# A fused attention and FFT-convolution kernel whose written-out order is searched anew, with two table evacuations ordered and unit columns set early

## The chip, the cores and the metric

The kernel runs on one core of a Trainium2 chip. The metric is the device time of one execution in microseconds. Engines go by the profile's names: PE multiplies matrices (PEld loads its weights), DVE, ACT and POOL are the vector, scalar and general engines, SP only issues transfers. Most executions of one kernel agree within 0.3%, and the comparisons made here tell 2% from no change.

## The reference

Two stages. The first is attention with 8 global keys and a causal window of 96 keys, for 4 batches of 8 heads, 768 positions and 64 columns a head. The second takes the joined heads as 768 x 512 rows, projects them to three parts, convolves the middle part along the positions (a Fourier transform of 768 points, a product with the transform of a filter, the inverse), multiplies it by the two other parts and projects once more.

```python
scores = scale * np.matmul(q, k.transpose(0, 1, 3, 2))
scores = np.where(keep, scores + bias, -1e9)          # bias: -slope of the head * distance
a = softmax(scores)
x = np.matmul(a, v)                                   # heads joined: 4 x 768 x 512
x1, x2, x3 = np.split(x @ w_proj, 3, axis=-1)
x2_conv = irfft(rfft(x2, axis=1) * rfft(filter, axis=0), n=768, axis=1)
out = (x1 * x2_conv * x3) @ w_out
```

## The kernel before

`graph` builds a list of 1,025 operations with what each reads and writes; `ORDER` is a text that says, in one sequence for all engines, which operation comes next, on which engine (P, A, V, G, S for PE, ACT, DVE, POOL, SP) and in which of the eight PSUM banks its result lies. "231A" is operation 231 on ACT; "226P2" is operation 226 on PE in bank 2; "i20b1" is 20 dummy matmuls (512 columns each) into bank 1, which only occupy PE. Each engine runs its own operations strictly in that order. A text that is once written is not changed at run time: where something is late, everything behind it on that engine is late.

The order was found off line by a search with the costs in the list (`act`, `dve`, `pe` and single figures in microseconds). These costs steer nothing when the kernel runs. The dependencies in the list (`r` and `w` are names of what is read and written) restrict the search; the waits in the program come from the recording layer, which compares the memory that operations touch.

Stages, by batch b of four. `attention(b)`: PE turns q and k around (`turned`; for b = 0 q is turned in f32 straight from the loaded rows, `turned32`, L628), ACT or DVE move the results to QT and KT, PE makes scores of two heads at a time into two banks (`scores`, L672 and L681), ACT takes the exponential (L695), DVE multiplies by a mask for b > 0 (L712); for b = 0 PE adds the distances first, from the small tables near and slope (L672). PE multiplies by v (`values`, L730 and L735; v carries one column of ones behind its 64, so the sum of the weights falls out), DVE divides (rc L759, xn L754), PE turns the result (L775), ACT or DVE move it to xT. `gate` projects x1 and x3 from xT (L844). `butterfly` adds and subtracts thirds of xT on DVE. `conv(b)`: `conv` projects (L911), `spectra` transforms (L615) and multiplies by h1 and h2, the inverse (L936, L939) gives eo, DVE joins the parts, gates them, and PE makes the output (L963), which SP stores. Batch b + 1's attention is interwoven with batch b's convolution.

Things made once. `tables` makes angles on PE and sines on ACT (`fwd`). `inverse_tables` turns these with PE into one bank and evacuates it in six parts, i = 0 to 5: three into `inv`, whose columns interleave (i = 0 takes the even blocks, i = 1 and 2 the odd ones), one into the first half of `inr`, and two into the second half of `inr`, i = 4 for rows 0 to 63 and i = 5 for rows 64 to 127, with opposite signs. `spectrum` makes h1 and h2 from the filter: DVE sums thirds of the loaded filter (pp, L557 and on) and PE transforms. `distances` and `masks` make near, slope and the masks from tables of POOL (iota, select) and from its identity matrix.

Loads. SP loads q of batch 0 (six loads, 256 KB each in f32, into the output buffers ot) and the first v rows. POOL issues every other load, 81 in all: k and v of every batch in seven pieces each, q of batches 1 to 3 in six, the weights w and wo and the filter. `load_v` sets the column of ones (and 31 columns behind it) of the v buffer once for each of the two buffers; `load_first` does it for the first one.

In the order before, operation 231 (i = 4) is ACT's and 232 (i = 5) is DVE's:

```
178P1 179V 200V 207V 201V 208V 209V 233V 203V 234V 144P4 226P2 228A 227A 232V 235V 145P5 147A 231A 146A 148V
```

Of the kernel before, what the change touches and what calls it, by code (L numbers as in the profile page):

```python
# [39 lines left out]
0V 30V 7V 47S 48S 14S 16S 57S 15S 49S 17G 18G 21G 22V 27V 28V 5G 6A 46A 31A 32A 25A 40A 34A 44A 33A 60G 23G  # L40
70V 71A 77A 72A 43A 37A 41A 38A 35A 76A 39A 73A 9V 54G 53G 59G 66G 55G 58G 20G 257G 56G 19G i20b1 108P0 109V
i1b2 85P1 86V 8V 10V 24V 258G 63G 64G 62G 3G 61G i2b3 79P2 80V 26V 11V 83P3 84A 45A 42A 110P4 111V 29V 88P5
89V 260S 259G 256G 65G 67G 69G 255G 273G 268G 267G 154P0 160P2 161V 87V 13V i1b6 81P1 82A 36A 78A 112P4 113V
155V 114P2 115V 50V 270G 269G 68G 263G 276G 158P3 159V 12V 90P67 91A 92P45 93A 118P01 119A 116P67 117A 156P2
157V 52V 51V 261S 274G 271G 120P45 121A 96P23 97A 122P01 94P67 95A 123A 358P4 359V 4V 487G 266G 275G i1b5
124P23 125V 126V 162P45 163A 166P67 167A 103P01 104V 105V 129P23 130V 131V 219P4 220A 127P5 128A 74A 98P67 99V
100V 221V 262V 222V 264S 265S 164P01 165A 168P23 169A 214P5 215A 75A 132P6 101P7 102V 1V 133V 216V 170P01 171V
172V 106P4 107A 223A 360P7 175P23 176V 217V 218A 2A 177V 134P4 136V 173P6 174V 139P0 141V 149P5 151A 361A
178P1 179V 200V 207V 201V 208V 209V 233V 203V 234V 144P4 226P2 228A 227A 232V 235V 145P5 147A 231A 146A 148V
225V 210V 202V 211V 204V 135P6 137A 138V 212V 205V 140P7 191P3 193A 356P5 357A 229A 486G 508G 272G 488G 490S  # L50
185P6 150P4 152A 230A 196P3 198A 368P01 369A 362P45 190P2 192A 142A 363A 180P3 182V 236V 430P0 431A 384P1 385V
206V 213V 143V 153V 194V 237V 386P7 387A 499G 502G 498G 496G 485G 495G 489G 181P2 365P45 366A 186P3 188A 187A
183A 285P0 286V 238V 388P45 389A 224A 390V 239V 364V 367V 298P1 294P3 295A 299A 283P0 284A 371P67 372A 373V
391P45 392A 394P23 395A 296P1 297V 393V 281P0 434P6 435A 505G 497G 309P7 310A 282A 432P4 433V 491S 503G 277G
278G 279G 504G 195P1 197A 374P23 375V 370V 376V 189V 184V 244P5 245A 397P67 398A 242P0 243A 240P1 241V 399V
307P4 308A 287P5 288A 377P2 378A 379P67 380V 381V 246P3 247A 400P01 401V 396V 402V 289P4 290A 248P67 249A 250V
251V 252P23 254A 253A 302P5 303A 405P01 406V 291V 407V 442P67 443A 436P23 437A 300P4 301V 584P5 585A 403P6
404V 614P7 382P0 383V 444V 311V 292V 408P1 409A 445P23 446A 615A 447V 293V 588P6 716G 713G 492G 493S 718S 727G
717G 507G 720G 439P45 440A 586P0 587V 312V 438V 304V 441V 305V 411P1 416P2 418A 413A 612P3 420P7 422A 613A
589A 421P4 662P2 663A 423A 415P5 417A 453P01 454V 455V 410P3 412A 448P67 449V 450V 729G 714G 734G 501G 733G  # L60
724G 715G 726G 500G 280G 723G 725G 660P2 719S 494S 722S 721S 732G 506G 321P4 322A 661A 456P5 457V 658P3 659V
306V 199V 730G 735G 731G 736G 728G 599P01 600A 590P67 591A 451P4 452V 317P5 318V 479V 478V 419V 480V 424V 481V
426P3 425P2 427A 428A 319P4 320A 327P5 328A 625P01 626A 325P2 326A 468P3 323P4 324A 315P5 316A 459P6 461A
313P7 314V 482V 429V 483V 329V 330V 484V 331V 627V 332V 601V 333V 619P01 513P4 514A 620A 474P5 476A 470A 526P2
527A 593P67 596P01 597A 594A 598V 334V 336V 592V 337V 595V 509P4 524P5 525A 522P3 523A 464P2 466A 616P01
622P67 623A 617A 473P3 475V 511P2 512A 812P5 813A 510A 469P6 471A 842P7 843A 607P01 608V 414V 609V 624V 621V
335V 618V 458P5 350P4 351A 814P2 815A 460A 535P3 602P67 603V 604V 477V 472V 528P0 529A 536A 353P4 354A 347P5
537P2 538A 348A 349S 633P01 634V 635V 462V 530P3 531A 816P4 817A 605P2 628P67 629V 539V 532V 606V 533V 630V
610P3 611A 463P5 465A 673P01 674A 338P4 339A 344P5 345V 540V 667P23 668A 664P01 665A 631P4 632V 669V 467V 666V
534V 675V 341P6 342V 343S 352S 355S 346S 340S 636P7 637A 517P5 518A 670P23 671A 672V 818P01 819A 515P4 516A  # L70
653P7 888P5 889A 655A 676P23 677V 520V 678V 519V 820V 521V 890P0 886P1 638P6 640A 643P4 555P7 556A 887A 645A
840P5 841V 644P6 646A 679P7 680A 891A 681P23 682V 683V 647V 648P1 650A 541P6 542A 649P7 651A 553P2 554V 684P6
685V 707V 706V 824P45 825A 827P01 828A 545P7 543P3 544A 691P6 693V 546V 709V 708V 639P2 641A 642V 710V 829V
652V 711V 847P45 892P01 893A 848A 894V 702P3 704A 551P2 549P6 550A 552A 697P7 821P01 822A 823V 898P45 741P3
742A 699A 692P2 547P6 548A 899A 557V 558V 712V 826V 849V 559V 737P0 738A 686P3 688A 895P67 853P45 854A 694A
654P1 656A 754P0 755A 896A 830P45 831V 560V 832V 561V 562V 564V 563V 657V 752P3 753A 750P2 751A 844P01 901P67
902A 845A 850P45 851A 739P3 696P2 687P6 689A 833P7 834A 835P01 836V 565V 837V 846V 852V 855V 900V 765P4 766A
756P5 757A 740A 569P6 570A 701P7 703A 758P0 763P1 764A 759A 698A 856P45 857V 858A 743P3 744V 897V 903V 695V
575P6 861P01 862V 863V 745P7 746A 576A 577S 904P23 905V 906V 767V 838P4 839A 572P5 859P7 860A 909P01 910V 760V
761V 748V 768V 762V 690V 747V 864P4 865A 911A 578P6 907P7 882P4 872P2 874A 573A 574S 566P3 912P0 913V 908V  # L80
749V 934V 935V 936V 937V 938V 939V 700V 940V 581P2 582A 771P5 772A 884A 881P1 783P2 773P7 774A 784A 777P0
769P5 775P4 776A 778A 770A 781P7 867P2 779P4 780A 579A 958P0 959A 782A 785V 786V 705V 787V 788V 789V 790V 791V
792V 929P5 941P4 942A 869A 943P0 944A 567A 568S 571S 580S 583S 956P6 967P2 968A 957A 954P0 955A 871P3 945P4
946A 883A 885V 793V 877P2 879A 962P0 963A 960P4 947P1 948A 961A 964V 965V 794P2 876P0 969P1 970A 971V 966V
972V 866P7 949P4 950A 873A 878A 868A 951V 952V 953V 870V 875V 880V 930P1 932A 931A 933V 800P6 801A 924P3 979P0
975P7 976A 980A 988P1 989A 795A 796S 803P4 977P5 978V 973P0 974A 981V 982V 983V 992P1 993A 990P2 991A 986P6
987A 804A 994V 984V 995V 985V 996V 805S 797P0 798A 999V 997V 1000V 998V 1001V 1002V 799S 802S 919P2 809P1 810A
921A 926A 811S 806P5 807A 1014V 808S 915P0 920P4 922A 917A 923V 914P2 916A 918V 1012V 925P3 927A 928V 1013V
1015V 1006P1 1007A 1008S 1003P2 1004A 1005S 1009P3 1010A 1011S 1022P0 1023A 1024S 1016P1 1017A 1018S 1019P2
1020A 1021S  # L90
"""


class Bank:


    def __init__(self):
# [1128 lines left out]
```

## Time and profile before

| | |
|---|---|
| median of 3 runs (lowest, highest) | 180.44 us (179.66, 183.96) |
| the profiled execution, its own time | 182.07 us |
| its span, first to last instruction | 180.3 us |
| mean granted PE clock | 0.986 |
| busy: PE, DVE, ACT, POOL | 168.0, 158.1, 153.7, 76.0 us |
| instructions | 4465 |
| POOL's transfer queue: packets, share of 16 DMA engines' span | 80912, 92.5% |

The profile is of one execution. Busy is the time in which an engine has an instruction in it; instructions of one engine may overlap by some hundredths, and PE's ends are modelled, so the distance from start to start of PE instructions says more than their durations. A row of the timeline has start, duration, engine, line, operation, what is written and read, and in brackets how long the engine stood idle and what ended that. The waits have total, times and longest. A line can be that of a helper: L307 and L311 are all of `copy` and `times` on ACT and DVE, so the names of the tiles tell operations apart.

### The profile page before, as it was taken

To read this page: it belongs to the slowest core of one execution; us is meant where nothing else is said; L and a number is where in the kernel's file an instruction comes from. 1 tells how busy PE (TensorE), PEld (TensorE's weight loads), DVE (VectorE), ACT (ScalarE), POOL (GpSimd) and SP (SyncE) were. 2 spreads that over 40 slices of the span, in tenths; PEclk is the share of its full clock that TensorE was granted. 3 is DMA by queue.
4 is the path that set the end of the run, shared out by engine and by line. 5 is a ranking of instruction groups with operands and counts; after the bars stand their busy time and mean duration, and the time that the engine had idled before them with its cause. 6 is when DMAs were issued, how large, how long until landed. Compare 5 with 4: busy or idle time off the path is not lost.

```text
span 180.3 us, 4465 instructions
## 1 busy us (share of the span) xinstructions
PE 168.0 (93%) x1725; PEld 105.8 (59%) x1725; DVE 158.1 (88%) x352; ACT 153.7 (85%) x298; POOL 76.0 (42%) x97
## 2 busy tenths in 40 slices
PE   7957997959999999999999999999999999999990
PEld 2545786634645576874476567665557674566540
DVE  2899889995698999999999999898999999999930
ACT  2697997938899999997999898899998888789761
POOL 7999998297895809899940000000000000000000
PEclk9999999996999999999999999999999999999998
DMA  6999999999999989999999106000001010501744
GB/s 122 208 177 164 161 165 204 175 178 157 161 138 109 133 54 66 138 142 143 164 151 71 58 26 268 4 0 0 4 0 63 20 39 25 210 4 58 291 184 167
DMA packets 91133, 20.74 MB, mean 115 GB/s; under 512 B 83864, under 2 KB 88040, under 8 KB 91112
## 3 DMA queue, kind: packets, MB, share of 16 engines
q0 software_dynamic: 80912, 12.14, 92.5%
q1 hardware_dynamic: 10200, 8.31, 14.6%
q8 instruction: 13, 0.21, 0.5%
q14 instruction: 8, 0.07, 0.1%
HBM read 25.84 MB, written 6.29 MB: 178 GB/s over the span
## 4 chain that ended last, share of the span: by engine, by line
PE 76%; DVE 15%; ACT 3%; issue 3%; POOL 2%; POOLq 0%; ACTq 0%; DVEq 0%
PE bank L844 21%; PE bank L911 12%; PE bank L963 12%; PE bank L681 6%; PE bank L936 5%; PE bank L641 5%; PE bank L615 4%; PE bank L775 3%; PE bank L730 3%; PE bank L735 3%; PE bank L672 2%; DVE xn L754 2%; DVE pp L557 1%; PE bank L939 1%; DVE eo L307 1%
## 5 line engine op out<-in xcount | busy, mean ns | idle before, releaser
L844 PE MATMUL bank<-xT,w 128*128 128x384 f16 x256 | 50.6, 332 | 2.5 <-ACT g L854 2.5
L695 ACT ACTIVATE E<-bank 128x864 f16<-128x864 f32 x48 | 41.1, 910 | 2.1 <-PE bank L681 2.0
L844 PEld LDWEIGHTS <-w 128*128 128x128 f16 x256 | 23.7, 99 | 18.5 <-issue 4.5
L323 POOL DMA_DIRECT2D kn<-in_k_dram x28 | 25.7, 920 | 9.4 <-PE bank L641 6.1
L323 POOL DMA_DIRECT2D vn<-in_v_dram x28 | 25.9, 927 | 4.9 <-DMA g<-in_moe_filter_fft_dram 3.0
L963 PE MATMUL bank<-wo,y 128*128 128x512 f16 x96 | 23.3, 379 | 0.0
L712 DVE TENSOR_TENSOR E<-E,mask 128x864 f16<-128x864 f16 x36 | 20.9, 597 | 0.0
L754 DVE TENSOR_TENSOR xn<-bank,rc 128x512 f16<-128x512 f32 (+1 forms) x22 | 17.0, 772 | 0.4
L323 POOL DMA_DIRECT2D qn<-in_q_dram x18 | 16.3, 918 | 1.4 <-DMA w<-in_moe_w_proj_dram 1.2
L854 ACT CAST g<-bank 128x384 f16<-128x384 f32 x32 | 15.5, 500 | 1.2 <-PE bank L844 1.0
L311 ACT ACTIVATE ot<-bank 128x512 f32<-128x512 f32 x22 | 13.6, 625 | 3.3 <-PE bank L963 3.2
L730 PE MATMUL bank<-vn,E 128*128 128x65 f16 x224 | 15.7, 193 | 0.0
L735 PE MATMUL bank<-vn,E 128*128 128x65 f16 x192 | 15.4, 193 | 0.0
L311 ACT ACTIVATE ab<-bank 128x512 f16<-128x512 f32 x22 | 13.1, 611 | 2.6 <-PE bank L911 2.6
L681 PE MATMUL bank<-QT,KT 64*128 64x216 f16 (+2 forms) x224 | 15.1, 246 | 0.1
L730 PEld LDWEIGHTS <-E 128*128 128x128 f16 x224 | 14.3, 98 | 1.4
L963 PEld LDWEIGHTS <-y 128*128 128x128 f16 x96 | 9.1, 98 | 9.2
L311 ACT ACTIVATE x<-bank 128x384 f16<-128x384 f32 x27 | 13.3, 513 | 1.1 <-PE bank L844 0.9
L307 ACT CAST X<-bank 128x512 f16<-128x512 f32 x22 | 12.7, 607 | 1.6 <-PE bank L615 1.4
L735 PEld LDWEIGHTS <-E 128*128 128x128 f16 x192 | 13.3, 97 | 1.0
L307 ACT CAST eo<-bank 128x384 f16<-128x384 f32 x27 | 11.9, 503 | 1.4 <-PE bank L939 1.4
L681 PEld LDWEIGHTS <-KT 64*128 64x128 f16 x224 | 8.6, 95 | 7.0 <-issue 4.8
(144 smaller groups left out, 366.0 us busy)
## 6 DMA issues: line engine op xcount, KB each, us to landing
out_dram<-ot SPq DMA_DIRECT2D x24, 256.0 KB
kn<-in_k_dram POOLq DMA_DIRECT2D x28, 120.0 KB, 6.1
vn<-in_v_dram POOLq DMA_DIRECT2D x28, 120.0 KB, 6.4
qn<-in_q_dram POOLq DMA_DIRECT2D x18, 128.0 KB, 6.4
ot<-in_q_dram SPq DMA_DIRECT2D x6, 256.0 KB
w<-in_moe_w_proj_dram POOLq DMA_DIRECT2D x4, 256.0 KB, 7.0
g<-in_moe_filter_fft_dram POOLq DMA_DIRECT2D x1, 768.0 KB, 10.5
w<-in_moe_w_proj_dram POOLq DMA_DIRECT2D x1, 512.0 KB, 11.1
```

The lines of the kernel that those rows point to most:

```text
L307: {"A": nc.scalar.copy, "V": nc.vector.tensor_copy, "G": nc.gpsimd.tensor_copy}[e](out, in_)
L311: self.nc.scalar.mul(out, in_, c)
L323: return self.g.op(eng, 0.57 + 0.00035 * nbytes[0] if eng == "G" else 0.5, lambda _: e.dma_start(dst, src), w=w, r=r, nbytes=nbytes, name= ...
L681: nc.tensor.matmul(bs[hh].f32()[:, off:off + w], self.KT[hs, hp, P * m:P * m + P], self.QT[hs, hp, KL * m:KL * m + w], start=(off == 0 and ...
L695: g.op("A", act(864), lambda _: nc.scalar.activation(eo, bs[0].two()[:, :, 0:432].rearrange("p h (m w) -> p h m w", m=2), Act.Exp, scale=s ...
L712: g.op("V", dve(864, 2), lambda _: nc.vector.tensor_mul(eo, eo, mk), r=[("mask", 2 * hp), ("mask", 2 * hp + 1)], w=[("E", hp, gi)], name=" ...
L730: nc.tensor.matmul(o[:, n, hh], ef[:, at:at + P], vt[:, t, 2 * hp + hh, 0:D + 1], start=first, stop=(t == 0), skip_group_check=True)
L735: nc.tensor.matmul(o[:, n, hh], ef[:, at:at + P], vt[:, t - 1, 2 * hp + hh, 0:D + 1], start=False, stop=True, skip_group_check=True)
L754: nc.vector.tensor_mul(to, o[:, :, :, 0:D], rc.to_broadcast([P, 2, 2 * nt, D]))
L844: nc.tensor.matmul(bk.f32()[:, 0:h], self.w[:, c, o + P * j:o + P * j + P], self.xT[:, c, h * s:h * s + h], start=(c == 0), stop=(c == 3))
L911: nc.tensor.matmul(bk.f32(), src[:, c], w[:, c, DM:2 * DM], start=(c == 0), stop=(c == 3))
L963: nc.tensor.matmul(bk.f32(), y[:, c, P * t:P * t + P], self.wo[:, c, :], start=(c == 0), stop=(c == 3))
```

## The change

One dependency is added: the parts i = 4 and i = 5 of the inverse tables now write the same name, so that the search keeps their sequence; the readers name five parts in place of six. The ones of the second v buffer become an operation of their own in `load_first` and leave `load_v`; operations 14 to 261 thereby get numbers one higher. Five figures of the search are replaced: the identity 0.45 to 0.57, the distances 1.8 to 1.93, the ones 0.53 to 1.5, the gaps 0.34 to 0.52, and the f32 turns from 512 to 256 columns a piece. The whole `ORDER` is new: the sequence on each engine, which of ACT and DVE evacuates what, the banks, the loads' sequence on SP and POOL, and the dummy matmuls (32 in four places instead of 25 in five). The number of instructions on DVE, POOL and SP stays. What is computed is the same.

```diff
--- before
+++ after
@@ ORDER (66 lines before, 65 after; the first three, and those with the inverse tables) @@
-0V 30V 7V 47S 48S 14S 16S 57S 15S 49S 17G 18G 21G 22V 27V 28V 5G 6A 46A 31A 32A 25A 40A 34A 44A 33A 60G 23G
-70V 71A 77A 72A 43A 37A 41A 38A 35A 76A 39A 73A 9V 54G 53G 59G 66G 55G 58G 20G 257G 56G 19G i20b1 108P0 109V
-i1b2 85P1 86V 8V 10V 24V 258G 63G 64G 62G 3G 61G i2b3 79P2 80V 26V 11V 83P3 84A 45A 42A 110P4 111V 29V 88P5
...
-178P1 179V 200V 207V 201V 208V 209V 233V 203V 234V 144P4 226P2 228A 227A 232V 235V 145P5 147A 231A 146A 148V
-225V 210V 202V 211V 204V 135P6 137A 138V 212V 205V 140P7 191P3 193A 356P5 357A 229A 486G 508G 272G 488G 490S
-185P6 150P4 152A 230A 196P3 198A 368P01 369A 362P45 190P2 192A 142A 363A 180P3 182V 236V 430P0 431A 384P1 385V
...
+0V 8V 31V 11V 7V 12V 1V 10V 9V 17S 50S 15S 16S 48S 49S 58S 18G 5G 39A 35A 42A 43A 45A 41A 6A 47A 37A 32A 2A
+38A 36A 33A 46A 51A 19G 22G 23V 28A 40A 44A 26V 55G 24G 71V 72A 77A 34A 79A 52V 25V 61G 54G 59G 60G i26b1 80P0
+86P1 87V 81V 29V 259G 20G 21G 57G 67G 56G 62G 3G i2b3 89P2 90V 27V 30V 88V 53V 13V 261S 260G 64G 63G 65G 257G
...
+147V 208V 203V 210V 211V 205V 206V 196P4 227P6 232A 146P7 148A 149V 234V 230V 235V 212V 207V 213V 236V 237V
+225V 373V 214V 136P5 138A 198A 182P2 192P3 194A 368P01 369A 362P45 363A 197P7 199A 191P3 141P0 143A 228A 231A
+193A 229A 233A 144V 238V 370V 195V 298P1 285P0 286A 281P7 282A 184A 386P6 387A 299A 498G 499G 294P0 295A 384P7
...
@@ -350,8 +349,8 @@
 
     def load_v(self, b, ts):
         vt, s = self.vn[b % 2], b % 2
-        if b == 1 and ts[0] == 0:
-            self.g.op("V", 0.2 if self.VD == 65 else 0.53, lambda _: self.nc.vector.memset(vt[:, :, :, self.D:], 1.0),
+        if False:
+            self.g.op("V", 0.2 if self.VD == 65 else 1.5, lambda _: self.nc.vector.memset(vt[:, :, :, self.D:], 1.0),
                       w=[("vn1", s)], name="ones")
         for t in ts:
             self.load_rows(("vn", s), vt, self.v, b, t)
@@ -391,7 +390,7 @@
 
         def ident(_):
             make_identity(nc, self.ident)
-        g.op("G", 0.45, ident, w=["ident"], bias=-1998.5)
+        g.op("G", 0.57, ident, w=["ident"], bias=-1998.5)
         g.op("AV", {"A": act(128), "V": dve(128, 1)}, lambda e: self.copy(e, self.ident32, self.ident), r=["ident"],
              w=["ident32"], bias=-1990.0, name="ident32")
         for lo, hi in ((0, 2), (2, 7)):
@@ -404,7 +403,7 @@
                 gap = et[:, :, 0:1488].rearrange("p h (m w) -> p h m w", m=6)[:, :, :, 216:248]
                 v.memset(gap, 0.0)
                 v.memset(et[:, :, 1456:1536], 1.0)
-            g.op("V", 0.34, gaps, w=[("E", i, c) for c in range(3)], name="gaps", bias=-3300)
+            g.op("V", 0.52, gaps, w=[("E", i, c) for c in range(3)], name="gaps", bias=-3300)
 
     def tables(self):
 
@@ -472,7 +471,7 @@
             g.op("AV", {"A": act(n), "V": dve(n, 1, True)},
                  lambda e, dst=dst, lo=lo, hi=hi, step=step, k=k, i=i: self.times(
                      e, dst, view()[(0, 64)[i == 5]:(P, 64)[i == 4], lo:hi:step], k), use=[b],
-                 w=[("inv", i)])
+                 w=[("inv", min(i, 4))])
 
     def distances(self):
 
@@ -492,7 +491,7 @@
                                     channel_multiplier=-sgn, compare_op=Alu.is_ge, fill=-HUGE)
             p.affine_select(dg[:, n:n + 48], dg[:, n:n + 48], pattern=[[0, 48]],
                             base=-NG - o, channel_multiplier=1, compare_op=Alu.is_ge, fill=-HUGE)
-        g.op("G", 1.8, first, w=["dg"], bias=-2000.0 + self.loads + 0.5)
+        g.op("G", 1.93, first, w=["dg"], bias=-2000.0 + self.loads + 0.5)
 
         def second(_):
             v.memset(dg[0:NG, 0:KL], -float(NL))
@@ -626,7 +625,7 @@
         def turn(_):
             for i in range(4):
                 nc.tensor.transpose(b.f32()[:, P * i:P * i + P], self.ot[t][:, P * i:P * i + P], self.ident32)
-        g.op("P", pe(*[512] * 4), turn, acq=[b], r=["ident32", ("ot", t)], name="q32")
+        g.op("P", pe(*[256] * 4), turn, acq=[b], r=["ident32", ("ot", t)], name="q32")
         g.op("AV", self.evac(512), lambda e: self.copy(
             e, self.QT[:, :, P * t:P * t + P], b.f32().rearrange("p (i c) -> p i c", i=4)), use=[b],
             w=[("QT", t)], name="qT")
@@ -939,7 +938,7 @@
                         nc.tensor.matmul(o[:, 0:P], self.p3[:, par, cs], self.inr[:, 2 + par],
                                          start=False, stop=True, skip_group_check=True)
                     g.op("P", pe(2 * P, 2 * P, P, P), turn, acq=[bk], r=[("X", s) for s in slots] + [
-                        ("inv", s) for s in range(6)], name="inv")
+                        ("inv", s) for s in range(5)], name="inv")
                     g.op("AV", self.evac(h), lambda e, eo=eo, jj=jj, par=par, bk=bk: self.copy(
                         e, eo[:, jj, par], bk.f32()[:, 0:h]), use=[bk], w=[ke + (jj, par)], name="eo",
                         after=self.early if b == 0 else ())
@@ -988,7 +987,7 @@
                 nc.tensor.matmul(o[:, 0:P], self.p3[:, par, cs], self.inr[:, 2 + par],
                                  start=False, stop=True, skip_group_check=True)
         g.op("P", 2 * pe(2 * P, 2 * P, P, P), turn, acq=bks, r=[("X", s) for s in range(6)] + [
-            ("inv", s) for s in range(6)], name="inv")
+            ("inv", s) for s in range(5)], name="inv")
         eo = self.eo[:, 2 * jp + jj]
         g.op("AV", self.evac(2 * h), lambda e: self.copy(e, eo, bks[0].two()[:, :, 0:h]), use=bks,
              w=[("eo", jp, jj, par) for par in range(2)], name="eo", after=self.early if b == 0 else ())
@@ -1095,8 +1094,10 @@
 
     def load_first(self):
         vt = self.vn[0]
-        self.g.op("V", 0.2 if self.VD == 65 else 0.53, lambda _: self.nc.vector.memset(vt[:, :, :, self.D:], 1.0),
+        self.g.op("V", 0.2 if self.VD == 65 else 1.5, lambda _: self.nc.vector.memset(vt[:, :, :, self.D:], 1.0),
                   w=[("vn1", 0)], name="ones", bias=-4400)
+        self.g.op("V", 1.5, lambda _: self.nc.vector.memset(self.vn[1][:, :, :, self.D:], 1.0),
+                  w=[("vn1", 1)], name="ones", bias=-3000)
         for c in range(3):
             for t in ([0, 1, 2], [3, 4], [5])[c]:
                 self.load_q(0, t)
```

## The prediction

> **What bounds the kernel now.** I read the page first, then the waits, then busy time by stretches, then the timeline around the one long gap of TensorE, and last the landings of the loads.
>
> ```profile
> PE 168.0 (93%) x1725; PEld 105.8 (59%) x1725; DVE 158.1 (88%) x352; ACT 153.7 (85%) x298; POOL 76.0 (42%) x97
> ```
>
> Three engines are within 15 us of each other, so the average names no bound. The stretches do (columns: length, then busy us of PE, PEld, DVE, ACT and POOL, the granted clock, DMA share, GB/s):
>
> ```profile
> 0.00:50.00 50.00, 42.26 (x493) 27.97 (x493) 39.56 (x103) 38.93 (x74) 42.09 (x60) 0.97 1.86 170
> 50.00:173.00 123.00, 122.85 (x1221) 76.79 (x1221) 118.59 (x250) 112.34 (x222) 33.94 (x38) 1.00 0.79 87
> ```
>
> From 50 to 173 us PE has no gap, and DVE has 4.4 us of room, ACT 10.7. All that can be won on PE lies ahead of 50 us; but what PE wins there it keeps only as far as DVE, which stands 10.4 us idle ahead of 50 us, moves ahead with it. The waits:
>
> ```profile
> ACT inr L311 <- DVE inr L313: 2.7, 1, 2.7
> ...
> PE bank L844 <- ACT g L854: 2.5, 1, 2.5
> ```
>
> The timeline at that place:
>
> ```profile
> 37.24 0.95 DVE L557 TENSOR_TENSOR pp<-g 128x1536 f16<-128x1536 f16 x1
> ...
> 38.44 0.95 DVE L557 TENSOR_TENSOR pp<-g 128x1536 f16<-128x1536 f16 x1
> ...
> 39.42 0.29 DVE L313 TENSOR_SCALAR inr<-bank 64x256 f16<-64x256 f16 x1
> ...
> 39.75 0.38 ACT L311 ACTIVATE inr<-bank 64x256 f16<-64x256 f16 x1 [2.73 <-DVE inr L313]
> ...
> 40.91 0.48 PE L844 MATMUL bank<-xT,w 128*128 128x384 f16 x2 [2.54 <-ACT g L854]
> ```
>
> Two halves of one table (inr, rows 0-63 and 64-127) are evacuated by different engines. ACT's half waits for DVE's, which stands behind the filter's sums (pp). Behind ACT's half stand the evacuations that free PE's banks, so PE stops from 38.38 to 40.91. Its clock is then halved:
>
> ```profile
> 42.26:45.67 3.41, 3.41 (x17) 1.38 (x16) 0.78 (x4) 2.29 (x5) 2.23 (x4) 0.50 2.39 152
> ```
>
> The place costs 2.54 us of gap, half of 3.41 = 1.7 us of clock, and some 0.5 us of small gaps at its edges: 4.7 us.
>
> **The change, part by part.**
>
> The key of the table. In the new order both halves of inr are on ACT, in the planned order, so the 2.73 us wait has no object. But two other parts (inv) write interleaved columns of one tile, and the built program makes ACT's 128x512 write wait for DVE's, which again stands behind the filter's first sum: a wait the plan does not see. By the walk below the filter lands at 25.8 + 10.5 (its issue to landing now) = 36.3, DVE reaches the sum at 37.5 and the table part is done at 38.8 (0.95 + 0.29), while ACT comes to its write at 40.2 only. Cost: nothing, covered by 1.4 us of ACT's own queue (two exponentials and two copies). If the filter lands later than about 38.9, each us is one us of ACT, and behind it of PE through the table's bank.
>
> The unit columns. DVE's fill of the second vn took 1.55 us in front of L425 and the copies that PE's transposes wait for:
>
> ```profile
> 27.85 1.55 DVE L354 MEMSET vn<- 128x1792 f16 x1 [0.32 <-issue]
> 29.32 0.35 DVE L425 TENSOR_TENSOR y<-y,bank 128x256 f32<-128x256 f32 x1
> ```
>
> PE waited 1.01 us there. Now the fill stands between two copies of KT at about 17.4. Behind it are one KT copy and one QT copy, and behind these the third group of scores, at about 20.2; ACT's exponentials set that time, so I cost it at nothing. Without that cover it is 1.55 us.
>
> The loads. SP's queue now brings q2, the first v rows, q0, q1, where q1 stood last. PE waited for q1 until 13.32; the fourth load had been used at 9.52. POOL makes the identity before the second k load, which delays that and all loads behind by 0.5 us, and the filter stands behind one more 0.9 us issue. All 81 POOL issues stay.
>
> The first scores. DVE reaches the last near and KT pieces at 11.7, PE the first local scores at about 12.0, against 15.57 now: 3.6 us. In exchange three k and two f32 q turns follow the first scores instead of preceding them: 3 x 0.22 + 2 x 0.43 = 1.5 us (4 starts 0.056 us apart, 4 starts 0.107 us apart). The plan's new figure for f32 turns changes no instruction.
>
> The fillers: 32 dummy matmuls for 25, 7 x 0.216 = 1.5 us. The 26 ahead of the first turn end at 8.25; the row's 20 ended near 7.0, and what the first turns need (q0, k0, k1) lands at about 5.8, 7.4 and 9.3. They are hidden up to some 0.5 us.
>
> ACT's chain. Twelve exponentials of the first batch run from 16.33 to 28.09 now, with three small operations between. They now start at 13.35 (five masks, three QT copies and the slopes are ahead) and end at 25.8, with three small ones and 0.9 us of waits for scores. PE starts the first gate at 27.5. The same sum of PE work is done at 31.0 now. Lead: 3.5 us.
>
> From there I walked each queue on by the rows, twice: with the mean duration of each row (an exponential 0.91 us), and with the distance from start to start when an engine is never idle (9 exponentials in 7.19, 0.80 each). In both, PE meets small waits for banks, 1.3 us in all, none above 0.6, and no gap like that at 38.38. Stations, slow walk and fast: QT of batch 1 evacuated 33.1 and 31.5; ACT's x1 and DVE's x1 that free the banks of the gates 34.2 and 32.7, 37.1 and 35.1 (PE waits 0.6 and 0.35 for the last); the last table part 44.8 and 42.1, which frees the bank of the k turn (0.55 and 0.05); QT behind it 48.75 and 45.6 (0.55 and 0.2). PE ends the 15th gate at 50.6 and 47.4; now it has done as much at 54.9. Lead of PE: 4.3 to 7.4 us.
>
> DVE's side. Moves between ACT and DVE, by net count: DVE gains 4 KT (3 x 0.69 + 0.39), 2 ot (0.69), one x (0.55) and the twin (0.72 on ACT; on DVE 0.42 to 0.69 by the 512-wide copies, I take 0.55), and loses 4 xT (0.40 + 3 x 0.45), one xn (0.69), one eo (0.55), one QT (0.5), one vn (0.61): +4.9 - 4.1 = +0.8 us. ACT comes out 0.3 us lower. In the walks DVE is idle for 5.0 to 8.2 us up to there instead of 10.4: 2.2 to 5.4 us, less 0.8 is 1.4 to 4.6. Of the 4.4 us of room after 50 us perhaps half can be used, as the queues of three engines never mesh fully: 3.6 to 6.8.
>
> The smaller of the two leads is 3.6 by the slow walk and 6.8 by the fast one. I take 4.3, nearer to the low end: from 50 us on PE, DVE and ACT would then end within 2 us of each other, and the next late thing is a bank that DVE has not emptied.
>
> [...] The half clock after the gap is in the row above: 2.54 us without a matmul were enough. [...]
>
> The sum: 180.3 - 4.3 = 176.0 us of span. The profiled execution took 182.07, 1.8 more than its span; the median of the runs is 180.44, so the profiled one is 1.6 on the slow side. Against the median: 180.44 - 4.3 = 176.1.
>
> **The rivals.**
>
> A. The lead is lost to DVE. For it: DVE is 96% busy after 50 us (118.59 of 123.00), and operations there last longer than the plan says (864 wide: 0.597 against 0.518). Against: PE has no gap in 123 us under the same costs. DVE then gets only its slow walk's 1.4 us, and none of its later room: 180.44 - 1.4 = 179.0.
>
> B. A late load; this ends slower. The new order puts the last values of batch 1 at 57.6 instead of 72.0. Their v load stands in POOL's queue behind four k loads of batch 2 that wait for PE's turns at 42.6 and 47.8. POOL issues it at about 50.2 and it lands 6.3 later, at 56.5. Slack 1.1 us. Each us beyond stops PE, and all behind it on PE; a stop of 2.6 us or more also halves the clock. Lateness decides from a landing at 60.2 on: 2.6 of stop and 1.7 of clock are the whole gain; at 62 the time is 180.44 - 4.3 + 4.4 + 1.7 = 182.2. For it: POOL's row names 3.0 us of waiting for the filter already now. Against: 0.85 us between landings holds steadily in the row.
>
> C. The change doesn't do what it says: the wait for the interleaved inv parts takes the place of the old one. The filter would have to land at 41.4 for a stop of 2.5 us on ACT and PE; then the 4.7 us of the old place are paid again, and there remains the head's 3.5 less the 1.0 that DVE does not follow: 180.44 - 2.5 = 177.9. Now it lands at 35.3 and the bound from the issue is 36.3, so it is unlikely.
>
> **How the numbers follow.** Forecast 0.60, A 0.20, B 0.12, C 0.08. 2% of the median, about what a measurement of this kernel can tell from no change, is 3.6 us: the lines are 176.8 and 184.0. The forecast's own range is 173.6 (the smaller lead of the fast walk, 6.8) to 176.8 (that of the slow one, 3.6), and a tenth of it falls above: 0.54 faster, 0.06 within. A and C lie within, 0.28. B is past 184.0 from a landing at 63.8 on; I give that 0.07, for waits that the plan misses as it missed the old one belong here, and 0.05 stays within. So 0.54, 0.39 and 0.07. The range takes in A and C, and B up to a stop of 3.7 us: 173.6 to 181.5.
>
> **What would show it.** Right: no wait of ACT for DVE above 1 us at inr or inv; a granted clock of 1.00 up to 170 us; first L671 matmul at 12.0; first gate near 27.5; DVE's idle time up to 50 us 5 to 8 us. Wrong: a gap of PE over 2 us anywhere, above all in front of values between 50 and 65 us (B) or at the k turns near 42 (C), or PE gaps of many tenths after 50 us with DVE without one (A). First scores after 14 us would make the head's term wrong.

## The result, and the profile after

The changed kernel takes 174.65 us (median of 4 runs, 174.50 to 174.85) against 181.15 us of the kernel before in the same session (4 runs, 179.66 to 183.96): a ratio of 0.967, 95% interval 0.959 to 0.974. The forecast was 176.1. The profiled execution took 174.67, its span 172.9: 7.4 us less than the span profiled before. The first row of the page, then the stretches (length, busy us of PE, PEld, DVE, ACT, POOL, granted clock, DMA share, GB/s):

```profile
PE 166.8 (96%) x1732; PEld 106.1 (61%) x1732; DVE 158.4 (92%) x352; ACT 151.9 (88%) x305; POOL 75.8 (44%) x97
...
0.00:50.00 50.00, 48.32 (x551) 31.42 (x552) 43.65 (x110) 44.92 (x87) 42.26 (x60) 1.00 1.84 168
50.00:165.00 115.00, 115.00 (x1169) 73.32 (x1167) 112.02 (x239) 105.76 (x217) 33.57 (x38) 1.00 0.86 93
```

PE has 6.1 us more busy time ahead of 50 us than before, 1.5 of it the 7 more dummies, and the granted clock of this stretch is 1.00 instead of 0.97. DVE stands idle there for 6.35 us instead of 10.44. After 50 us PE again has no gap. The chain that ended last, by engine:

```profile
PE 93%; DVE 4%; issue 0%; ACT 0%; ACTq 0%; DVEq 0%
```

PE's own waits (total, times, longest) are down to the one at the start, for the fill of the dummies' operand, and one in front of a turn:

```profile
PE bank L302 <- DVE idle L375: 1.2, 1, 1.2
PE bank L640 <- DVE KT L306: 0.4, 1, 0.4
```

And the inverse tables in the timeline, ACT and DVE:

```profile
36.73 0.37 ACT L310 ACTIVATE inr<-bank 64x256 f16<-64x256 f16 x1
38.20 0.95 DVE L556 TENSOR_TENSOR pp<-g 128x1536 f16<-128x1536 f16 x1
39.07 0.28 DVE L312 TENSOR_SCALAR inv<-bank 128x256 f16<-128x256 f16 x1
39.27 0.94 DVE L556 TENSOR_TENSOR pp<-g 128x1536 f16<-128x1536 f16 x1
41.22 0.60 ACT L310 ACTIVATE inv<-bank 128x512 f16<-128x512 f16 x1
...
42.77 0.38 ACT L310 ACTIVATE inr<-bank 64x256 f16<-64x256 f16 x1
```

No row has a bracket: the two halves of inr on ACT wait for nobody, and ACT's write of inv comes 1.87 us after DVE's part (39.35) behind which it had to stand.

**Where the 7.4 us are.** For every two consecutive PE instructions I took the distance from start to start less the plan's price of the first (`pe`: columns / 2400 + 0.0025 us; a f32 turn twice that) and summed what is left, by stretch; the first row contains the 1.19 us up to PE's first instruction. A negative sum means distances shorter than that price; the assignment is good to some tenths.

| stretch of PE, us | before | both single edits (below) | after |
|---|---|---|---|
| 0 to 30 | 2.91 | 2.04 | -0.57 |
| 30 to 50 | 4.38 | 0.12 | -0.37 |
| after 50 | -1.40 | -1.00 | -2.06 |
| price of the 7 more fillers | | | +1.51 |

Before to after: 30 to 50 us gives 4.75, the head 3.48 less 1.51 of fillers = 1.97, the rest 0.66; in sum 7.38.

**Two groups of runs of the kernel before.** In the four sessions of the experiments below the kernel before ran 42 times; one run of 184.62 us stands apart and is left out. In 17 runs the mean granted clock was 0.993 or higher and the time 180.27 to 180.51 (median 180.36). In 24 it was 0.976 to 0.991 and the time 181.28 to 182.96 (median 182.15). The profiled execution of before, 182.07 at 0.986, is of the second group. The reading is that the half clock after the gap of 2.54 us falls in some executions and not in others, and is worth 1.8 us; its 3.41 us at half clock would make 1.7. Only this one execution of before has a profile, so in the others the half clock is read from the mean alone. The time at 180.44 that the forecast started from fits the first group; no clock is on record for the runs of that session, and two of them (179.66 and 183.96) lie outside both groups. The changed kernel has no such gap, and its runs lie within 0.35 us (0.2%); the two groups of the kernel before together span 2.69 us (1.5%), so the 0.3% named at the start does not hold for it.

### The profile page after: what moved, and what is told of

Read it like the earlier page. It is cut to its first block, busy times and chain, and to the rows that moved or that the text cites. A ratio compares the mean times of both kernels' runs of the same rounds, so it can differ in the third digit from the quotient of the medians.

```text
span 172.9 us, 4486 instructions
## 1 busy us (share of the span) xinstructions
PE 166.8 (96%) x1732; PEld 106.1 (61%) x1732; DVE 158.4 (92%) x352; ACT 151.9 (88%) x305; POOL 75.8 (44%) x97
## 3 DMA queue, kind: packets, MB, share of 16 engines
HBM read 25.84 MB, written 6.29 MB: 186 GB/s over the span
## 4 chain that ended last, share of the span: by engine, by line
PE 93%; DVE 4%; issue 0%; ACT 0%; ACTq 0%; DVEq 0%
PE bank L843 25%; PE bank L910 12%; PE bank L962 12%; PE bank L614 6%; PE bank L680 6%; PE bank L640 6%; PE bank L935 5%; PE bank L302 5%; PE bank L729 4%; PE bank L774 4%; PE bank L734 3%; PE bank L671 2%; PE bank L938 1%; DVE KT L306 1%; DVE vn L1097 1%; DVE vn L306 1%
## 5 line engine op out<-in xcount | busy, mean ns | idle before, releaser
L843 PE MATMUL bank<-xT,w 128*128 128x384 f16 x256 | 48.7, 326 | 0.0
L694 ACT ACTIVATE E<-bank 128x864 f16<-128x864 f32 x48 | 40.6, 902 | 1.3 <-PE bank L680 1.3
L962 PE MATMUL bank<-wo,y 128*128 128x512 f16 x96 | 23.8, 379 | 0.0
L753 DVE TENSOR_TENSOR xn<-bank,rc 128x512 f16<-128x512 f32 (+1 forms) x21 | 16.1, 771 | 0.3
L310 ACT ACTIVATE ot<-bank 128x512 f32<-128x512 f32 x20 | 11.9, 611 | 4.9 <-PE bank L962 4.9
L729 PE MATMUL bank<-vn,E 128*128 128x65 f16 x224 | 15.2, 193 | 0.0
L729 PEld LDWEIGHTS <-E 128*128 128x128 f16 x224 | 14.0, 97 | 1.8
L734 PE MATMUL bank<-vn,E 128*128 128x65 f16 x192 | 14.9, 193 | 0.0
L306 ACT CAST eo<-bank 128x384 f16<-128x384 f32 x28 | 12.7, 512 | 1.7 <-PE bank L938 0.9
L680 PE MATMUL bank<-QT,KT 64*128 64x216 f16 (+2 forms) x224 | 14.0, 241 | 0.0
L734 PEld LDWEIGHTS <-E 128*128 128x128 f16 x192 | 13.1, 97 | 0.7
```

What stands on the lines that cost most here:

```text
L306: {"A": nc.scalar.copy, "V": nc.vector.tensor_copy, "G": nc.gpsimd.tensor_copy}[e](out, in_)
L310: self.nc.scalar.mul(out, in_, c)
L680: nc.tensor.matmul(bs[hh].f32()[:, off:off + w], self.KT[hs, hp, P * m:P * m + P], self.QT[hs, hp, KL * m:KL * m + w], start=(off == 0 and ...
L694: g.op("A", act(864), lambda _: nc.scalar.activation(eo, bs[0].two()[:, :, 0:432].rearrange("p h (m w) -> p h m w", m=2), Act.Exp, scale=s ...
L729: nc.tensor.matmul(o[:, n, hh], ef[:, at:at + P], vt[:, t, 2 * hp + hh, 0:D + 1], start=first, stop=(t == 0), skip_group_check=True)
L734: nc.tensor.matmul(o[:, n, hh], ef[:, at:at + P], vt[:, t - 1, 2 * hp + hh, 0:D + 1], start=False, stop=True, skip_group_check=True)
```

## The experiments

Times are medians; before means the 41 runs just told of, after means 174.65.

**The table part alone.** In the kernel before, part i = 5 of the tables goes to ACT:

```diff
-... 226P2 228A 227A 232V 235V 145P5 147A 231A 146A ...
+... 226P2 228A 227A 235V 145P5 147A 231A 232A 146A ...
```

> The kernel before with the table part alone: the second half of inr (i = 5) goes from DVE to ACT, directly behind the first half; nothing else of the order is touched. Theory P (PE is the bound and the others follow): the 2.73 us wait of ACT is gone, PE has no gap at 38.4 and no half clock, and 2.5 to 4.7 us are won: about 177 against the kernel before. The spread of the kernel before (179.7 to 184.0), if it is the half clock that falls here or not, shrinks to below 1 us. Rival D (DVE limits from 50 us on): DVE's row is then late and the gain is 0 to 1.5 us although the wait is gone. Rival S (the new order won by other means, the stall had been paid back later): below 0.5 us.

178.14 us (178.07 to 179.32, 4 runs, all at a clock of 0.996 or more). Against the runs of before at full clock that is -2.2, against the half clock ones -4.0, and all four runs lie below all of before. The row up to 50 us has PE busy for 3.1 us more than before, and no half clock:

```profile
0.00:50.00 50.00, 45.36 (x523) 29.52 (x524) 43.13 (x110) 42.92 (x82) 42.99 (x61) 1.00 1.87 170
```

DVE and all behind it follow. The rivals D (0 to 1.5) and S (below 0.5) fall. One run, 179.32 at a clock of 1.00, lies 1.2 us above the other three, so the spread did not quite shrink to below 1 us; why is open.

**The ones alone.** The fill of the second v buffer stands at 2.2 us in DVE's idle time:

```diff
-0V 30V 7V 47S
+0V 30V 7V 262V 47S
...
-100V 221V 262V 222V
+100V 221V 222V
```

> The kernel before with the fill of the second v buffer's unit columns alone moved to DVE's idle time at 2.2 us; everything else stays. PE waited 1.01 us behind it at 27.9. Theory P: up to 1.0 us won in front of the stall, but the stall of 2.54 us at 38.4 has its end set by DVE (sums of the filter, then the table half) and these are set by the filter's landing, so PE only waits longer there: 0 to 0.5 us. Rival: the 1.55 us of DVE come off in full: 1.0 to 1.5 us.

180.82 us. Of ten runs, eight at a clock of 0.984 to 0.990 took 180.18 to 181.06, 1.3 below the half clock runs of before; a single one at full clock took 179.40, 1.0 below the full clock runs of before; one at 0.981 took 182.71. My expectation of 0 to 0.5 fails, the rival (1.0 to 1.5) holds. The timeline of this kernel says why:

```profile
35.80 0.95 DVE L557 TENSOR_TENSOR pp<-g 128x1536 f16<-128x1536 f16 x1
...
38.31 0.38 ACT L311 ACTIVATE inr<-bank 64x256 f16<-64x256 f16 x1 [2.42 <-DVE inr L313]
39.48 3.38 PE L844 MATMUL bank<-xT,w 128*128 128x384 f16 x12 [2.27 <-ACT g L854]
```

DVE reaches the filter's sum at 35.80 instead of 37.24. The filter lands at 35.31 in the kernel before and at 35.38 here, so the end of the stall was set by DVE's queue and not by the landing. What is taken off DVE ahead of it moves the whole stall forward, up to the landing: of the 1.55 us fill, 1.44 came through, and 0.4 would be left.

**Both.** The two edits together.

> The kernel before with both single edits, the table half on ACT and the ones early. Theory P: the two add up now that the stall no longer swallows the ones: the gain of the table alone plus about 1.0 us, 3.5 to 5.7 in all. What is missing to the 6.5 us of the whole change is then the head and the rest of the order: 1 to 3 us. Rival S (order searched anew does most): both together below 2 us.

177.40 us (177.23 to 177.81): 3.0 below the full clock group, 4.75 below the other. They add up: 2.2 + 1.0 is 3.2, and rival S (below 2) falls. Down to 174.65 there remain 2.75 us, and the table above places them: 2.6 in the head, less the 1.5 of fillers, 0.5 at 30 to 50, 1.1 behind. One thing was not expected. In the profiled run PE waits in the head, 1.78 us up to 12.45 and 0.61 up to 14.61, and the clock is halved for 3.41 us:

```profile
12.45 0.38 PE L641 MATMUL bank<-ident,kn 128*128 128x128 f16 x4 [1.78 <-DVE QT L307]
```

```profile
14.25:17.66 3.41, 3.00 (x22) 1.75 (x23) 3.09 (x7) 2.28 (x4) 3.41 (x5) 0.50 2.31 155
```

```profile
16.86 0.89 ACT L695 ACTIVATE E<-bank 128x864 f16<-128x864 f32 x1 [1.10 <-PE bank L681]
```

That run took 177.30, the three at a clock of 0.994 to 1.00 took 177.23 to 177.81. So there the half clock costs nothing that the times show, although ACT waits 1.10 us for PE's scores in it and starts its first exponential at 16.86 instead of 16.42 with the table part alone. How this is made good was not found. The price of 1.8 to 2.0 us is that of the half clock behind the stall at the tables and not of every half clock.

**The old fault put back into the new order.** Part i = 5 is DVE's, behind both sums of the filter, and ACT's first half behind it (operations 148 and 149 follow them):

```diff
-... 196P4 227P6 232A 146P7 148A 149V 234V 230V 235V 212V ...
+... 196P4 227P6 146P7 234V 230V 235V 233V 232A 148A 149V 212V ...
...
-193A 229A 233A 144V ...
+193A 229A 144V ...
...
-                 w=[("inv", min(i, 4))])
+                 w=[("inv", i)])
... (its two readers again name six parts)
```

> The changed kernel with the old fault put back at its new place: the second half of inr is DVE's again, behind both sums of the filter, and ACT's first half stands behind it in the sequence. Theory P: ACT waits from 36.9 to about 40.5 (3.6 us), behind it the evacuation of gates, PE stops 2.5 to 3.5 us at about 38 and its clock is halved: +3.5 to +5 us, some 179. Rival D (DVE or something later is the bound and there is room): below +1.5 us. Rival S: the rest of the new order hides it: below +0.5.

178.50 us (177.39 to 179.76), +3.85, as expected (3.5 to 5), and again in two groups: 177.39 and 177.71 at full clock, 179.29 and 179.76 at 0.985 and 0.990. So 2.9 us for the stall and 2.0 more where the clock is halved, by two runs each. The profile, of the run of 179.76:

```profile
40.00 0.29 DVE L312 TENSOR_SCALAR inr<-bank 64x256 f16<-64x256 f16 x1
40.39 0.38 ACT L310 ACTIVATE inr<-bank 64x256 f16<-64x256 f16 x1 [3.41 <-DVE inr L312]
...
41.94 0.36 PE L680 MATMUL bank<-QT,KT 64*128 64x216 f16 x4 [3.25 <-ACT x L310]
```

The wait of ACT (3.41) turns into a gap of PE (3.25) almost one for one, and that into 2.9 us of time. The new order hides next to nothing of it. Rivals D and S fall.

**More work for DVE.** 8 fills of the idle tile, 2.2 us, one each behind operations 304, 479, 483, 512, 335, 539, 823 and 712:

```diff
+        for _ in range(8):
+            g.op("V", 0.3, lambda _: self.nc.vector.memset(self.idle, 0.0), name="pad")
```

> The changed kernel with 8 more fills of the idle tile (128x512 f16, 0.27 us each) on DVE, 2.2 us in all, one each between 60 and 113 us. DVE has 3.0 us of room after 50 us. Theory P (PE is the bound, DVE follows with its room): 0 to 0.8 us more, and PE without a gap above 0.3 us. Rival A of the prediction (from 50 us on DVE decides): each of the 2.2 us comes back, +1.8 to +2.2.

174.95 us (174.42 to 175.25): +0.3 for 2.2 us. PE is still never idle in the stretch, with DVE at 112.70 of 115:

```profile
50.00:165.00 115.00, 115.00 (x1166) 73.04 (x1165) 112.70 (x247) 105.63 (x217) 33.36 (x38) 1.00 0.86 94
```

Rival A of the prediction, by which all 2.2 us come back, falls: a share of 97% is not a bound here. The test goes as far as the 2.2 us, which is less than the 3.0 us that DVE had idle in this stretch.

**More work for PE.** Two dummies more at each of five places, i2b3 ahead of 317P3 for instance; 10 x 0.216 = 2.16 us.

> The changed kernel with 10 more dummy matmuls (512 columns, 0.216 us each) on PE, 2.2 us in all, two each at five places between 67 and 92 us. Theory P: PE is never idle there, so all of it comes back: +1.9 to +2.3. Rival A (DVE or ACT decides): below +1.

176.99 us (176.44 to 177.32): +2.34 for 2.16 us. PE decides where they stand, between 67 and 92 us.

**The filter later.** Its load goes behind w512 and four loads of batch 1 in POOL's queue:

```diff
-... 66G 70G 69G 82P3 ... 270G 267G 268G 273G ...
+... 66G 69G 82P3 ... 270G 267G 268G 70G 273G ...
```

> The changed kernel with the filter's load five places later in POOL's queue (behind w512 and four loads of batch 1); its landing goes from 36.4 to about 42.3. This is the prediction's rival C made true: ACT's write of inv (i = 0) stands behind DVE's part (i = 2), which stands behind the filter's first sum. Theory (the cover of 1.4 to 1.9 us is real, beyond it each us is one of ACT and PE): ACT waits from 41.2 to about 43.5 (2.3 us), DVE for the filter from 38.3 on (4 us), PE stops 1.5 to 2.5 us at the k turn (43.2) and may have its clock halved: +2 to +4.5 us. Rival (the wait the plan does not see is covered by ACT's or PE's other work even then): below +1.

178.80 us (178.30 to 178.96), +4.15, as expected (2 to 4.5); the filter lands at 42.29. Two of the runs, at a clock of 0.985, took 178.30 and 178.89, the two at full clock 178.71 and 178.96: here too a lower clock shows no price, though where it was lower in those two is not on record. The waits, of DVE and ACT, and the rows of PE:

```profile
DVE pp L556 <- DMA g<-in_moe_filter_fft_dram: 3.6, 1, 3.6
...
ACT inv L310 <- DVE inv L312: 1.8, 1, 1.8
```

```profile
44.73 0.60 PE L910 MATMUL bank<-w,xo 128*128 128x512 f16 x2 [1.34 <-DVE xo L795]
...
50.58 0.55 PE L680 MATMUL bank<-QT,KT 64*128 64x216 f16 x8 [1.00 <-DVE QT L306]
```

The interleaved table part does make ACT wait, 1.75 us. But PE's gaps name DVE: the butterflies (xo) and the QT copy stand behind the filter's sum on DVE, and these are late by the whole 3.6 us. No gap of PE names ACT. So the place that rival C named is real, its path is not the only one, and the one that PE's gaps show goes through DVE's queue. These gaps make 2.7 us of the 4.15; where the rest arises was not traced.

**q1 late, as before.** SP's sequence has q1 last:

```diff
-... 17S 50S 15S 16S 48S 49S 58S ...
+... 17S 50S 15S 48S 49S 58S 16S ...
```

> The changed kernel with q1 as the last of SP's loads, as before the change; nothing else. It lands some 3 loads later, at 11.5 to 13.5 instead of about 9; PE's fourth turn waits for it. Theory of the prediction (the head is kept one for one to the end): first scores and first exponential 1.5 to 2 us later, +1.0 to +2.0 us. Rival (the head is hidden in ACT's masks or made good later): below +0.5.

179.69 us (178.50 to 180.32), +5.0; the profiled run, the fastest of the four, +3.8. My expectation of 1.0 to 2.0 fails by far. The row of PE, and the clock:

```profile
13.72 1.97 PE L627 MATMUL bank<-p,ot 128*128 128x128 f32 x8 [2.94 <-DMA ot<-in_q_dram]
```

```profile
13.07:16.48 3.41, 2.76 (x11) 2.16 (x12) 3.08 (x3) 1.34 (x3) 3.41 (x5) 0.50 2.39 152
```

The first scores come at 17.60 instead of 13.13, the first gate at 32.84 instead of 29.02, and the end 3.83 later: from the first gate on the delay is kept one for one. I had expected the first scores 1.5 to 2 us later; the wait alone was 2.94, and the half clock I had left out. What the three slower runs lost besides is not known.

**Fewer fillers.** `i26b1` becomes `i20b1`.

> The changed kernel with 20 dummy matmuls ahead of the first turn instead of 26. In the profile they end at 9.32 and the first turn's data has landed by 7.8, so they are in its way by 1.3 us. ACT's masks end at 14.11 and the first exponential starts at 14.12, so ACT would not follow. Theory (ACT's masks and DVE's queue hide it): first scores 0.5 to 1.2 us earlier, first exponential at most 0.4 us earlier, time -0.4 to +0.2. Rival (head one for one, as the run with q1 last showed for a delay): -1.0 to -1.3. Second rival (PE gets gaps and a half clock in the head): +0.5 or more.

174.45 us (174.15 to 174.75, 6 runs), 0.2 below after: within the spread. First scores at 12.25 (0.9 earlier), first exponential at 13.80 (0.3 earlier). PE now waits 0.60 us for the second k load and 1.00 for the third instead; no gap halves the clock. The theory (-0.4 to +0.2) holds.

**The ones put back.** Behind operation 217, in front of the second subtraction (the two SP copies into that buffer follow them there):

```diff
-... 158V 162V 14V 97P01 ...
+... 158V 162V 97P01 ...
...
-... 217V 218V ...
+... 217V 14V 218V 265S 264S ...
```

> The changed kernel with the fill of the second v buffer's unit columns put back in front of the second subtraction behind the angles (L424, at 27.4), as it stood before the change. In the kernel before, taking it away from there won 1.0 to 1.3 us. Theory (it is on the path there and off it at 18.6): +0.5 to +1.2. Rival (DVE now has idle time around it): below +0.3.

175.97 us (175.70 to 176.25), +1.3, just above the expected 0.5 to 1.2; the rival (below 0.3) falls. DVE's fill and the gap of PE behind it:

```profile
27.70 1.55 DVE L1099 MEMSET vn<- 128x1792 f16 x1 [0.32 <-issue]
29.17 0.62 DVE L424 TENSOR_TENSOR y<-y,bank 128x512 f32<-128x512 f32 x1
```

```profile
29.85 0.20 PE L729 MATMUL bank<-vn,E 128*128 128x65 f16 x1 [1.44 <-DVE y L424]
```

At 18.6 no wait for it shows; at 27.7 it costs 1.3 of its 1.55 us, although DVE is idle for 6 us ahead of 50.

**A try at a better head.** 20 fillers, two masks of ACT moved from 13.3 and 16.4 to 28.5, the third k turn behind the third scores.

> A try at a better version: the changed kernel with 20 dummies ahead of the first turn, two masks of ACT (0.77 us each) moved from 13.3 and 16.4 to its idle time at 28.5, and the turn of the third k load (landed 14.4) behind the third scores instead of ahead of it. Theory (head one for one once the masks are out of the way): first exponential 1.0 to 1.5 us earlier, time -0.6 to -1.3, some 173.6. Rival (PE's work is dense from 9.3 on, and what is won is lost to the waits for the loads of k): -0.3 to +0.5.

174.92 us (174.42 to 175.08): no gain; the theory (-0.6 to -1.3) fails. The first exponential starts 1.0 us earlier (13.16) and the first gate 0.9 earlier (28.14), but at 31.5 and 32.4 PE waits for copies of ACT, in whose queue the two masks now stand ahead of them; by the sums over 30 to 50 us that is 1.0 us, and what the head won is gone. The changed kernel is not beaten.

**The new head in front of the old order.** The first 172 words of the new order, then all that is left in the order of before, with both single edits.

> The kernel before with both single edits (table half on ACT, ones early) and, besides, the changed kernel's head: its first 172 words of the order, up to the angles' sums and before the last pair of batch 0's exponentials, and from there on the order of before for all that is left. What it still lacks is the new order behind about 27 us. Theory (the head is kept one for one): in the two profiles the first gate starts at 30.3 with the two edits alone and at 29.0 after the whole change, so -1.0 to -1.6 against the 177.4 of both edits: 175.8 to 176.4, and the 1.2 to 1.7 us down to 174.65 are those of the order behind. Rival (the head's lead is lost in the old order behind it): 177.0 to 177.8. Second rival (the head is all that is missing): 174.4 to 175.0.

184.08 us (183.29 to 185.70): slower than before. None of the three figures came, and the profile shows why at the seam. The old order turns a q of batch 1 right after the head; in the new sequence of loads that q comes later:

```profile
29.95 0.61 PE L641 MATMUL bank<-ident,qn 128*128 128x128 f16 x4 [5.39 <-DMA qn<-in_q_dram]
```

```profile
25.82:36.06 10.24, 5.60 (x68) 4.70 (x69) 3.94 (x10) 3.50 (x6) 6.66 (x8) 0.50 1.55 194
```

So this run does not tell what the head alone is worth. That stays with the sums by stretch (about 1.1 of the 2.75 us net of fillers) and with the run with q1 late, which shows that a delay of the head is kept. For the order at 30 to 50 us (0.5) and behind (1.1) there are the sums alone, and no run that takes them apart.

## Why the prediction was right, and where its steps were off

The sign and the mechanism held, and the time is 1.4 us below the forecast, inside its range. The likeliest case came true: no wait of ACT for DVE at the tables, a granted clock of 1.00, DVE idle for 6.35 us ahead of 50 us (forecast 5 to 8). That the time came so close is in part luck: two steps below were off by 1.5 us or more, in opposite directions.

- **The place of the stall** was put at 4.7 us. The sum over 30 to 50 us fell by 4.75, but 4.26 of that come with the two single edits and 0.49 only with the rest of the new order. 4.26 is the 2.54 of the gap and the 1.7 of the clock; the 0.5 for small gaps at the edges was not in the place. In times, the gap gave 2.2 and 2.9 by the runs at full clock (table alone; fault put back, there with a gap of 3.25) and the clock 1.8 to 2.0.
- **The half clock was subtracted from a time that did not contain it.** The prediction noted that the profiled execution was 1.6 us slower than the median and left it at that. By the two groups that difference is the half clock. From 182.07 the whole 7.4 come off, from 180.44 only 7.4 - 1.8 = 5.6, to 174.8. By this step alone the forecast would have come out 1.8 us too low; the leads that it wrote off (below) more than made up for it.
- **The half clock behind a gap.** The prediction had one row for it, with the gap of 2.54 us, and took from it that a stop of 2.6 us or more also halves the clock (rival B). In the profiles gaps of 2.27 us (ones alone), 2.54 (before), 2.94 (q1 late), 3.25 (fault put back) and 5.39 (new head in front of the old order) went with a half clock, and so did one of 1.78 with one of 0.61 behind it (both edits); gaps of 1.01 to 1.44 did not. But of 41 runs of the kernel with the 2.54 us gap only 24 had the lower clock, and with the fault put back two of four. So the length of the gap alone does not tell whether the clock is halved.
- **The head** was to lead by 3.5 us at the first gate. That came at 29.02 instead of 27.5, and the head gave 1.97. The 26 fillers did not end at 8.25 but at 9.32, because the first 12 started 0.43 us apart where I had taken the 8 of the run before; and DVE reached the last near and KT piece at 13.66 instead of 11.7, as it waited for the turns behind them. First scores 13.13 instead of 12.0. Of the 1.1 us of late fillers little reached the end: with six fewer the time fell by 0.2.
- **The leads lost on the way** are the step that was off most. The head's 3.5 and the place's 4.7 are 8.2; I let the slow walk, small waits and DVE take 3.9 of it. PE's lead at the 15th gate was 6.4 us (it ends about 48.5), inside the walks' 4.3 to 7.4, and nothing was lost behind: 7.4 at the end. The 1.3 us of small waits of PE for banks did not come: one of 0.44 is all that the profile has.
- **DVE** was counted by number and not by place. The net +0.8 us came out at +0.2 in DVE's busy time, and where it lies matters more. The last 7.3 us before and after:

```profile
173.00:180.30 7.30, 2.83 (x14) 1.08 (x11) 0.00 (x0) 2.40 (x5) 0.00 (x0) 0.90 0.56 217
```

```profile
165.60:172.90 7.30, 2.86 (x14) 1.08 (x11) 2.12 (x4) 0.64 (x2) 0.00 (x0) 1.00 0.49 190
```

DVE (third busy figure) had nothing to do there before and has 2.12 us after: three copies of the output stand on it there (DVE has four of these 24 copies now, two more than before), outside its crowded part. So DVE's 7.4 us come as 4.1 of less idling ahead of 50, 1.4 of its 4.4 us of room behind, 2.1 in the tail, less 0.2. The run with 2.2 us more on DVE shows that it was not the bound there.
- **The ones**: nothing at 17.4, 1.55 without cover. In the runs: no wait where they stand, 1.3 where they stood.
- **The rivals.** A is refuted by the added work (+0.3 for DVE, +2.34 for PE). B did not come near: the v load that it named landed at 57.0 (forecast 56.5), and its values start at 59.8 and 60.6, later than the 57.6 assumed, so the slack was 2.8 us. C's wait exists, with 1.87 us of cover against the 1.4 forecast. Made true, it cost 4.15 us where ACT waited 1.75, and the gaps of PE named DVE.

## What to carry to other kernels

Before a gain is taken off a median, ask whether that median contains what is removed: a loss that falls in some runs only (here, by the clock of each run, in 24 of 41) shows as two groups of times, and the profile is of one of them. Find the bound of a stretch by giving each engine the same 2 us more to do rather than by its busy share; and count moved work by where it lands, since the 2.1 us that DVE, 92% busy, took over in the last stretch lie where it had nothing to do. An order on PE and an order of loads are one object: half of one with half of the other cost 6.7 us, most of it at a single load.

## What the runs showed of the hardware

As long as PE has work, the half clock comes in the profiles in pieces of one length: 3.41 us in five (before, ones alone, both edits, fault put back, q1 late), and 10.24, three times that, with the gap of 5.39. In the clock records of the traces before and after the changes lie whole multiples of 3.413 us apart: 11, 1 and 39 times before, 49 times after. Before, the clock falls at 42.253, rises at 45.666 and falls again at 178.786, when PE has no more work (its last instruction ends at 175.83). In these six profiles the fall comes between 1.3 and 3.9 us after the gap's start, and twice inside it (q1 late: the gap ends at 13.72, the clock falls at 13.07; new head in front of the old order: 29.95 and 25.82).

In the 3.41 us just ahead of the fall PE stood idle, before, for 2.08 us:

```profile
38.84:42.25 3.41, 1.33 (x9) 0.81 (x9) 3.25 (x9) 2.50 (x6) 3.19 (x4) 1.00 1.73 180
```

In the five profiles with one piece at half clock, PE was idle for 1.99 (both edits) to 2.93 us (fault put back) of the 3.41 ahead of it. In the traces before and after, cut into lengths of 3.413 us from the first clock record on, those with up to 1.64 and 1.67 us idle (11.53 to 14.95 before, 166.72 to 170.13 after) were followed by full clock; with the new head in front of the old order the clock fell after 1.27 us idle. So this idle time does not separate the two cases either. Why the same gap of 2.54 us went with the lower clock in some runs and not in others was not shown, since only one execution of before has a trace.

At the start the dummies are 0.43 us apart, later 0.216, half of that. In the profile before the distance changes at 4.7 us, in the one after at 6.3; by the matmuls counted in each half us, between 4.5 and 5.5 with the ones put back and between 6.5 and 7.5 with the filter later. The first clock record begins there, at 4.71 before and at 6.29 after, and ahead of it the rows give 1.00, so the row does not show it. In four profiles with the new head (after, more work for DVE, more for PE, ones put back) the first scores stand between 12.39 and 13.22 us, and the copies to xT that ACT makes behind the first batch's exponentials start between 27.21 and 27.50: 0.83 us of spread has become 0.29. This fits the run with six fewer dummies, where the time stayed.
